# The second chunk's first pair of weight tiles as eight plain block products

## The chip, the cores and the metric

The kernel runs on one core of one Trainium2 chip. The metric is the device time of one execution in microseconds (us), lower is better. A core has five queues that run side by side: TensorE (PE, matmuls; its weight loads are a row of their own, PEld), VectorE (DVE), ScalarE (ACT), GpSimd (POOL) and SyncE (SP), which here issues every DMA transfer. Each runs its own instructions strictly in order and waits where an operand of another queue isn't ready.

## The reference

```python
q_s = np.exp(q - np.max(q, axis=-1, keepdims=True))      # then divided by its sum over the 64 features
k_s = np.exp(k - np.max(k, axis=2, keepdims=True))       # then divided by its sum over the 576 positions
kv = np.einsum('bhsd,bhse->bhde', k_s, v)                # 8 batches x 8 heads, 64 x 64 each
x = np.einsum('bhsd,bhde->bhse', q_s, kv)                # then seen as 4608 tokens x 512
a = x @ w_a                                              # 512 x 1536
b = x @ w_b
return (a * b @ w_out).astype(np.float32)                # 1536 x 512
```

q, k and v are float32; the three weights arrive as 64-bit floats.

## The kernel before, in words

**Tiles.** The tokens go through in nine chunks of 512. For each chunk, attention gives x, transposed (512 features x 512 tokens, four tiles of 128 features). d_ff = 1536 is cut into 12 blocks of 128 (f = 0 to 11) or six pairs (i = 0 to 5). For a pair, TensorE makes a and b (the gate products, line 535 of the profile, `product`), the product a\*b is formed by ACT and DVE, and is multiplied with the pair's rows of w_out (line 556, `project`), summed over all pairs in four accumulators `po`.

**Precision.** An operand is split into a high and a low part (`split`: ACT casts the high part at line 79, DVE subtracts it at line 82), and a product is three matmuls: high x high, high x low, low x high. The first chunk's w_out products (line 545, `project_first`) are single f32 matmuls.

**First chunk (c = 0).** It is computed plainly (line 510), while the weights are loaded, turned from 64-bit to f32 (`float_parts`: ACT, DVE, a POOL add at line 110, DVE), split, and put into scratch in device memory: the f32 tile of each half block as `dy`, and of three of a pair's four half blocks (A11, A12, A22: block f = 2i or 2i+1, first or second half of the 512 features) the split tile as `dw` (`keep_ab`, `put_w`).

**Later chunks.** A pair is made by Winograd's form of Strassen's scheme: x is cut into 2 x 2 blocks (B11, B21: first and second half of the features for the first half of the tokens; B12, B22 for the second), the weights into A11, A12, A21, A22, and seven products of sums replace eight. `x_operands` makes the sums of x (T1 to T4, tiles `xt`, lines 483 to 494) and splits all seven operands into tiles `xo`. `sums(i)` loads the four `dy` of a pair and makes the weight sums S1 to S4 on POOL (line 225). In chunk 1 the sums are split there and then, used, and put into `dw`; chunks 2 to 8 load all seven tiles of a pair from `dw` with `get_w` into eight buffers `ws`. The seven results are combined on DVE (tiles u2, u3, cc).

**Around the boundary of chunks 0 and 1.** `sums(0)` is called in chunk 0's last block, `sums(1)` at the start of chunk 1's pair 0. `x_operands` for chunk 1 goes through B11, T2, T3, T1, B21, B22, T4. The first PSUM banks of chunk 1 (k0 for `kx`, k1 for `ky` and `kp`) are those that the last gate products of chunk 0 (`pt`) leave: k0 is free after ACT's copy at line 517, k1 after DVE's product at line 521. In the same place an attention task for a later batch runs (`pm`, `mc`, `m`, `pmx`: a column maximum turned on TensorE and spread back, lines 261 to 276).

**What sets the order.** A scheduler of the language orders each queue when the program is built, from the order of the code, a timeline of its own and a few pinned places (`issue_after`, and the hand-written list of start steps). So an edit in one place can reorder instructions far from it.

Of the kernel before, what the change touches and what calls it, by code (L numbers as in the profile page):

```python
# [20 lines left out]

A11, S2, S3, S1, A12, S4, A22 = range(7)
B11, T2, T3, T1, B21, B22, T4 = range(7)
P1, P6, P7, P5, P2, P3, P4 = range(7)


# [1 line left out]
def linear_attention_then_gated_ffn(  # L30
# [162 lines left out]
    def keep_ab(f, half, y, w):  # L193
        i, r = divmod(f, 2)
        dy[i, r, half] = dr.tile([P, DM], F32, name=f"dy{i}{r}{half}")
        nc.sync.dma_start(out=dy[i, r, half], in_=y)
        op = ((A11, A12), (None, A22))[r][half]
        if op is not None:
            put_w(i, op, w)
        blocks[f, half] = w  # L200

# [4 lines left out]
    def get_w(i, op):  # L206
        w = ws_tile()
        nc.sync.dma_start(out=w.bitcast(F32), in_=dw[i, op].bitcast(F32))
        return w

    def sums(i):

        a = {}
        for r in range(2):
            for h in range(2):
                a[r, h] = sb.tile([P, DM], F32, name="ws_y", tag="wy", bufs=8)
                nc.sync.dma_start(out=a[r, h], in_=dy[i, r, h])
        sub, add = ALU.subtract, ALU.add
        for o, x, y, op in (
            ((1, 1), (1, 0), (1, 1), add),  # L220
            ((1, 0), (0, 0), (1, 0), sub),
            ((0, 0), (1, 1), (0, 0), sub),
            ((0, 1), (0, 1), (0, 0), sub),
        ):
            nc.gpsimd.tensor_tensor(out=a[o], in0=a[x], in1=a[y], op=op)
        return {S1: a[1, 1], S3: a[1, 0], S2: a[0, 0], S4: a[0, 1]}
# [249 lines left out]
    def x_operands(xf, which, box):  # L476

        b11, b12 = xf[:, 0:2, 0:H], xf[:, 0:2, H:T]
        b21, b22 = xf[:, 2:4, 0:H], xf[:, 2:4, H:T]
        for op in which:  # L480
            if op == T2:
                t1, t2 = t_tile(), t_tile()
                nc.vector.tensor_tensor(out=t1, in0=b12, in1=b11, op=ALU.subtract)
                nc.vector.tensor_tensor(out=t2, in0=b22, in1=t1, op=ALU.subtract)
                box["t1"], box["t2"] = t1, t2
                src = t2
            elif op == T3:
                src = t_tile()
                nc.vector.tensor_tensor(out=src, in0=b22, in1=b12, op=ALU.subtract)
            elif op == T1:  # L490
                src = box["t1"]
            elif op == T4:
                src = box["t2"]
                nc.vector.tensor_tensor(out=src, in0=b21, in1=src, op=ALU.subtract)
            else:
                src = {B11: b11, B21: b21, B22: b22}[op]
            o = xo_tile([P, 2, 2, H])
            split(o[:, 0], o[:, 1], src)
            box[op] = o
# [508 lines left out]
    for f in range(2, NF):  # L1008
        if 1 < f - 1 < NF - 3:
            tasks[f - 1][0]()  # L1010
        if f + 2 < NF:
            load_f(f + 2)

        with tc.issue_after(at["end", f - 2].ins):
            convert_wo(f)
            if f + 1 < NF:
                convert_ab(f + 1, 0)
                convert_ab(f + 1, 1)


        n = f - 3
        if n < 0:
            copies = ()
        else:
            copies = tasks[n][2]()
        if n + 1 < NF - 3:
            with tc.issue_after(startup[0]), tc.issue_after(at["end", max(f - 2, 1)].ins):
                tasks[n + 1][1]()
        if f == NF - 1:
            with tc.issue_after(at["end", f - 1].ins):  # L1030
                split_wo(0)
                split_wo(1)
            sy[0] = sums(0)
        if f > 2:
            pts = gate_banks(("k0", "k1"))
            for h in range(2):
                gate_part(f, x0, h, range(NP), pts[h])
                if h == 0:
                    with ExitStack() as pinned:
                        for copy in copies or ():  # L1040
                            pinned.enter_context(tc.issue_after(copy.ins))
                        at["ga", f] = gate_half(f, pts[0])
            at["end", f] = gate_end(at["ga", f], pts[1])
        if 0 <= n < len(tasks):
            tasks[n][3]()
        if f == NF - 2:
            x_operands(xfs[1], early + late, xo)
        project_first(*pending, po)
        pending = (f, at["ga", f])
    in_order((E.PE,), by_hand, len(traced))  # L1050
# [2 lines left out]
    def run_pending(last_only=False):  # L1053

        if not pend:
            return
        f, ghl, c, po = pend.pop(0)
        if c:
            project(f, ghl, po, c == NCH - 1 and f >= NF - 2)
        else:  # L1060
            project_first(f, ghl, po)
        if f == NF - 1:
            store(c, po)

    last = None
    for c in range(1, NCH):
        more = c + 1 < NCH
        attend = Spread(attention_tasks(c + 1) if more else [], 3 * NI - 3 - (1 if c == 1 else 0))
        po = None
        x, xo = xo, {}  # L1070
        for i in range(NI):
            def operand(op):
                if c > 1:
                    return get_w(i, op)
                if op in (A11, A12, A22):
                    return get_w(i, op)
                w = split_w(sy[i][op])
                put_w(i, op, w)
                return w

            if more and i == NI - 1:
                x_operands(xfs[c + 1], early, xo)
            kx = ps.tile([P, 2, H], F32, name="kx", tag="k0")
            ky = ps.tile([P, 2, H], F32, name="ky", tag="k1")
            ka = ps.tile([P, 2, H], F32, name="ka", tag="k2")
            cc = sb.tile([P, 4, 2, H], F32, name="cc", bufs=1)
            u2 = sb.tile([P, 2, H], F32, name="u2", bufs=1)
            u3 = sb.tile([P, 2, H], F32, name="u3", bufs=1)
            if c > 1 or i > 0:
                attend(last)  # L1090
            if c == 1:
                if i + 1 < NI:
                    sy[i + 1] = sums(i + 1)
                    split_wo(2 * i + 2)
                    split_wo(2 * i + 3)
            product(kx, operand(A11), x[B11], True)
            product(ky, operand(S2), x[T2], True)
            nc.scalar.copy(out=u2, in_=kx)  # L1098
            nc.vector.tensor_tensor(out=u2, in0=ky, in1=u2, op=ALU.add)  # L1099
            product(ka, operand(S3), x[T3], True)  # L1100
            last = nc.vector.tensor_tensor(out=u3, in0=ka, in1=u2, op=ALU.add)
            if more and i == NI - 1:
                x_operands(xfs[c + 1], late, xo)
            end = c == NCH - 1 and i == NI - 1
            if not end:
                run_pending()
            attend(last)
            kp = ps.tile([P, 2, H], F32, name="kp", tag="k1")
            product(kp, operand(S1), x[T1], True)
            product(kx, operand(A12), x[B21], False)  # L1110

            nc.vector.tensor_tensor(out=cc[:, 3], in0=kp, in1=u3, op=ALU.add)  # L1112
            nc.scalar.copy(out=cc[:, 0, 0], in_=kx[:, 0])  # L1113
            nc.vector.tensor_tensor(out=cc[:, 0, 0], in0=kx[:, 1], in1=cc[:, 0, 0], op=ALU.mult)
            last = nc.vector.tensor_tensor(out=cc[:, 3, 0], in0=cc[:, 3, 0], in1=cc[:, 3, 1], op=ALU.mult)
            if not end:
                run_pending()
            if po is None:
                po = [ps.tile([P, DM], F32, name=f"po{t}") for t in range(TT)]
            attend(last)  # L1120
            product(kp, operand(S4), x[B22], False)
            nc.vector.tensor_tensor(out=cc[:, 1], in0=kp, in1=u2, op=ALU.add)  # L1122
            nc.vector.tensor_tensor(out=cc[:, 1, 0], in0=cc[:, 1, 0], in1=cc[:, 1, 1], op=ALU.mult)  # L1123
            g1 = g_split(2 * i, cc[:, 0:2, 0])
            last_product = product(ka, operand(A22), x[T4], False)
            nc.vector.tensor_tensor(out=cc[:, 2], in0=ka, in1=u2, op=ALU.add)
            last = nc.vector.tensor_tensor(out=cc[:, 2, 0], in0=cc[:, 2, 0], in1=cc[:, 2, 1], op=ALU.mult)
            g2 = g_split(2 * i + 1, cc[:, 2:4, 0])
            pend += [(2 * i, g1, c, po), (2 * i + 1, g2, c, po)]
# [53 lines left out]
```

## Time and profile before

| | |
|---|---|
| runs | 973.65 us median of 3 (969.36 to 974.25) |
| profiled execution, first to last instruction | 970.9 us; what lies around it isn't recorded apart |
| TensorE busy | 941.8 us, 97% |
| VectorE, ScalarE, GpSimd busy | 631.3, 392.7, 104.2 us |
| DMA | 282.6 MB, mean 291 GB/s |
| chunk 0's last gate product starts its last 24 matmuls | 145.09 us |
| first matmul of chunk 1 | 155.17 us |
| first matmul of chunk 2 | 271.91 us |

Times within the execution count from the first instruction. In a timeline a row is a run of equal instructions: start, duration, engine, line, operation, output<-inputs, shapes, count, and in brackets the idle time before it and what ended it. A matmul's shown duration includes its way through the array; the pace of a row of matmuls is the distance of their starts. In the chain of waits a row's duration is that pace.

### The profile page before, as it was taken

The numbers are of one execution on the slowest core, as the hardware profiler recorded it, in microseconds if no ns is written. First come the engines' busy times: TensorE is split into PE (matmuls) and PEld (weight loads), VectorE is DVE, ScalarE is ACT, GpSimd is POOL, SyncE is SP. The second block draws the span as 40 slices with busy tenths as digits, with TensorE's granted clock in tenths as the row PEclk, the third lists the DMA queues.
The fourth block names the chain that finished last, engine by engine and source line by source line (L and its number), as shares of the span: only waits on it lengthen the run. The fifth ranks groups of instructions, "written<-read, shape, count | busy, mean of one in ns | idle before, by whom it ended". The sixth has DMA issues, their size and how long they took to land.

```text
span 970.9 us, 16970 instructions
## 1 busy us (share of the span) xinstructions
PE 941.8 (97%) x6159; PEld 844.9 (87%) x6159; DVE 631.3 (65%) x1249; ACT 392.7 (40%) x1085; POOL 104.2 (11%) x88
## 2 busy tenths in 40 slices
PE   5889998999999999999999999999999999999998
PEld 4656766899999999999999999999999999999997
DVE  7987878886686747665666657665766546553433
ACT  7787654543372416232443235223522263221101
POOL 1544343422000000000000000000000000000000
PEclk9999999999999999999999999999999999999999
DMA  9999585989998968997799779977998688767761
GB/s 347 411 383 377 203 291 183 410 308 344 302 347 274 373 232 274 302 378 245 255 332 358 260 251 334 322 268 256 337 296 289 240 299 269 275 226 273 255 208 59
DMA packets 97586, 282.60 MB, mean 291 GB/s; under 512 B 11680, under 2 KB 12256, under 8 KB 97504
## 3 DMA queue, kind: packets, MB, share of 16 engines
q1 hardware_dynamic: 97504, 281.52, 81.8%
q8 instruction: 49, 0.80, 0.3%
q14 instruction: 33, 0.27, 0.1%
HBM read 241.40 MB, written 37.98 MB: 288 GB/s over the span
## 4 chain that ended last, share of the span: by engine, by line
PE 87%; DVE 5%; DMA 2%; issue 2%; ACT 1%; POOL 1%; SPq 1%; DVEq 0%; POOLq 0%; ACTq 0%
PE po L556 27%; PE kp L535 14%; PE kx L535 14%; PE ka L535 13%; PE ky L535 7%; PE pk L312 3%; PE pt L510 3%; PE po L545 2%; PE px L466 2%; DMA raw<-in_w_ab 1%; POOL wr L110 1%; DMA mr<-dq 1%; DVE wy L113 1%; PE px L454 1%; DVE wo_w L82 0%
## 5 line engine op out<-in xcount | busy, mean ns | idle before, releaser
L556 PE MATMUL po<-wo_w,gh 128*128 128x512 f32 x768 | 231.0, 396 | 0.0
L535 PE MATMUL kx<-xo,ws 128*128 128x256 f32 x1152 | 164.7, 284 | 4.3 <-ACT ga L517 4.3
L556 PEld LDWEIGHTS po<-wo_w,gh 128*128 128x128 f32 x768 | 138.9, 189 | 26.4 <-ACT gh L79 0.3
L535 PE MATMUL ka<-xo,ws 128*128 128x256 f32 x1152 | 161.2, 283 | 0.0
L535 PE MATMUL kp<-xo,ws 128*128 128x256 f32 x1152 | 157.9, 284 | 1.4 <-DVE u L1099 1.4
L535 PEld LDWEIGHTS kx<-xo,ws 128*128 128x128 f32 x1152 | 151.0, 190 | 7.1 <-ACT ga L517 4.7
L535 PEld LDWEIGHTS ka<-xo,ws 128*128 128x128 f32 x1152 | 149.8, 188 | 3.9 <-issue 0.5
L535 PEld LDWEIGHTS kp<-xo,ws 128*128 128x128 f32 x1152 | 147.9, 190 | 3.9 <-issue 1.6
L556 PE MATMUL po<-wo_w,gl 128*128 128x512 f32 x384 | 140.1, 395 | 0.0
L79 ACT CAST gh<-cc 128x512 fp32r<-128x512 f32 x96 | 57.6, 621 | 135.6 <-DVE cc L1123 127.6
L1122 DVE TENSOR_TENSOR cc<-kp,u 128x512 f32<-128x512 f32 x48 | 33.2, 691 | 103.9 <-PE kp L535 103.9
L1113 ACT COPY cc<-kx 128x256 f32<-128x256 f32 x48 | 17.8, 372 | 189.4 <-PE kx L535 183.3
L556 PEld LDWEIGHTS po<-wo_w,gl 128*128 128x128 f32 x384 | 71.5, 188 | 16.4 <-DVE gl L82 0.4
L380 ACT ACTIVATE qt<-qt,st 128x64 f32<-128x64 f32 x224 | 75.0, 338 | 22.5 <-DVE st L377 16.3
L1112 DVE TENSOR_TENSOR cc<-kp,u 128x512 f32<-128x512 f32 x48 | 32.9, 686 | 73.3 <-PE kp L535 73.1
L535 PE MATMUL ky<-xo,ws 128*128 128x256 f32 x576 | 77.7, 284 | 0.6 <-DVE cc L1122 0.3
L535 PEld LDWEIGHTS ky<-xo,ws 128*128 128x128 f32 x576 | 72.0, 189 | 1.5 <-DVE cc L1122 0.5
L510 PE MATMUL pt<-xo,ws 128*128 128x512 f32 x288 | 70.3, 400 | 1.1 <-DVE ws L925 1.1
L82 DVE TENSOR_TENSOR gl<-cc,gh 128x512 fp32r<-128x512 f32 x96 | 65.4, 688 | 8.1 <-ACT gh L79 8.1
L510 PEld LDWEIGHTS pt<-xo,ws 128*128 128x128 f32 x288 | 53.5, 189 | 13.9 <-DVE ws L925 1.5
L244 POOL PARTITION_ALL_REDUCE mx<-m x20 | 14.4, 722 | 459.6 <-DVE m L255 432.1
L1098 ACT COPY u<-kx 128x512 f32<-128x512 f32 x48 | 28.0, 584 | 82.0 <-PE kx L535 82.0
(144 smaller groups left out, 1197.9 us busy)
## 6 DMA issues: line engine op xcount, KB each, us to landing
ws<-dw SPq DMA_DIRECT2D x312, 512.0 KB, 5.3
dw<-ws SPq DMA_DIRECT2D x42, 512.0 KB, 6.8
mr<-dq SPq DMA_DIRECT2D x112, 128.0 KB, 4.4
raw<-in_w_ab SPq DMA_DIRECT2D x24, 512.0 KB, 7.6
out<-ot SPq DMA_DIRECT2D x36, 256.0 KB, 4.6
vt<-in_v SPq DMA_DIRECT2D x28, 325.0 KB, 7.6
qt<-in_q SPq DMA_DIRECT2D x32, 256.0 KB, 5.2
kt<-in_k SPq DMA_DIRECT2D x24, 320.0 KB, 5.1
```

The lines of the kernel that those rows point to most:

```text
L79: nc.scalar.copy(out=hi, in_=src)
L82: return nc.vector.tensor_tensor(out=lo, in0=src, in1=hi.bitcast(F32), op=ALU.subtract)
L312: nc.tensor.matmul(pk, kt[:, j].rearrange("p h d -> p (h d)"), vt[:, j], start=(j == 0), stop=(j == J - 1),)
L380: nc.scalar.activation(out=qt[:, j, h], in_=qt[:, j, h], func=AF.Exp, bias=st[:, h, 0, j:j + 1], accum_out=st[:, h, 1, j:j + 1],)
L466: nc.tensor.matmul(px[:, s], w, m[:, s], start=(i == 0), stop=(i == 2))
L510: nc.tensor.matmul(pt, w[:, wp], x[g][:, xp], start=(g == 0 and i == 0), stop=(g == NP - 1 and i == 2),)
L535: ins = nc.tensor.matmul(pt[:, n], w[:, n, wp, c], x[:, xp, c], start=(first and n == 0 and i == 0), stop=(i == 5), skip_group_check=True,)
L545: nc.tensor.matmul(po[t], g[:, t * P:(t + 1) * P], wo_first[f], start=(f == 0), stop=(f == NF - 1),)
L556: ins = nc.tensor.matmul(po[t], a[:, ts], wo[f][:, w], start=(f == 0 and i == 0), stop=(f == NF - 1 and i == 2),)
L1098: nc.scalar.copy(out=u2, in_=kx)
L1112: nc.vector.tensor_tensor(out=cc[:, 3], in0=kp, in1=u3, op=ALU.add)
L1122: nc.vector.tensor_tensor(out=cc[:, 1], in0=kp, in1=u2, op=ALU.add)
```

## The change

- Pair 0 of chunk 1 is made by eight plain block products: A11·B11 + A12·B21, A11·B12 + A12·B22, A21·B11 + A22·B21 and A21·B12 + A22·B22, each result a\*b formed by a new helper `plain_gate` (ACT copies a, DVE multiplies with b).
- For that, A21's split tile of pair 0 is put into `dw` during chunk 0 as well and pair 0 loads four tiles with `get_w`; x needs an eighth operand, B12.
- `x_operands` for chunk 1 makes the plain blocks first (B11, B21, B12, B22) and the sums T2, T3, T1, T4 after.
- `sums(0)` is called in pair 4 of chunk 1, and the four weight sums of pair 0 are split and put into `dw` in pair 5, for chunks 2 to 8, which are computed as before.

```diff
-A11, S2, S3, S1, A12, S4, A22 = range(7)
-B11, T2, T3, T1, B21, B22, T4 = range(7)
+A11, S2, S3, S1, A12, S4, A22, A21 = range(8)
+B11, T2, T3, T1, B21, B22, T4, B12 = range(8)
...
-        op = ((A11, A12), (None, A22))[r][half]
-        if op is not None:
+        op = ((A11, A12), (A21, A22))[r][half]
+        if op != A21 or i == 0:
             put_w(i, op, w)
...
-                src = {B11: b11, B21: b21, B22: b22}[op]
+                src = {B11: b11, B12: b12, B21: b21, B22: b22}[op]
...
-            sy[0] = sums(0)
...
-            x_operands(xfs[1], early + late, xo)
+            x_operands(xfs[1], (B11, B21, B12, B22, T2, T3, T1, T4), xo)
...
+    def plain_gate(to, pt):
+
+        nc.scalar.copy(out=to[:, 0], in_=pt[:, 0])
+        return nc.vector.tensor_tensor(out=to[:, 0], in0=pt[:, 1], in1=to[:, 0], op=ALU.mult)
...
-            ky = ps.tile([P, 2, H], F32, name="ky", tag="k1")
+            ky = None if c == 1 and i == 0 else ps.tile([P, 2, H], F32, name="ky", tag="k1")
...
                 if i + 1 < NI:
                     sy[i + 1] = sums(i + 1)
+                if i + 2 == NI:
+                    sy[0] = sums(0)
+                if i + 1 < NI:
                     split_wo(2 * i + 2)
                     split_wo(2 * i + 3)
+                else:
+                    for op in (S2, S3, S1, S4):
+                        put_w(0, op, split_w(sy[0][op]))
+            if c == 1 and i == 0:
+                kp = ps.tile([P, 2, H], F32, name="kp", tag="k1")
+                w = get_w(i, A11)
+                product(kx, w, x[B11], True)
+                product(kp, w, x[B12], True)
+                w = get_w(i, A12)
+                product(kx, w, x[B21], False)
+                last = plain_gate(cc[:, 0], kx)
+                product(kp, w, x[B22], False)
+                last = plain_gate(cc[:, 1], kp)
+                run_pending()
+                attend(last)
+                po = [ps.tile([P, DM], F32, name=f"po{t}") for t in range(TT)]
+                g1 = g_split(0, cc[:, 0:2, 0])
+                w1, w2 = get_w(i, A21), get_w(i, A22)
+                product(ka, w1, x[B11], True)
+                product(ka, w2, x[B21], False)
+                last = plain_gate(cc[:, 2], ka)
+                kx = ps.tile([P, 2, H], F32, name="kx", tag="k0")
+                attend(last)
+                product(kx, w1, x[B12], True)
+                product(kx, w2, x[B22], False)
+                last = plain_gate(cc[:, 3], kx)
+                g2 = g_split(1, cc[:, 2:4, 0])
+                pend += [(0, g1, c, po), (1, g2, c, po)]
+                continue
```

The scheduler makes other queues of it. Three places, each before and with the change.

**TensorE at the boundary of chunks 0 and 1**, from chunk 0's last gate products (`pt`) on. Before:

```order
L510 MATMUL pt_1411<-xo,ws 128x512 x12
L510 MATMUL pt_1412<-xo,ws 128x512 x12
L535 MATMUL kx<-xo,ws 128x256 x12
L271 MATMUL pmx<-m_1391,ones 128x128
L545 MATMUL po_492<-wo_w,ga 128x512
```

With the change:

```order
L510 MATMUL pt_1404<-xo,ws 128x512 x12
L510 MATMUL pt_1405<-xo,ws 128x512 x12
L535 MATMUL kx<-xo,ws 128x256 x13
L271 MATMUL pmx<-m_1396,ones 128x128
L545 MATMUL po_494<-wo_w,ga 128x512
L545 MATMUL po_495<-wo_w,ga 128x512
L545 MATMUL po_496<-wo_w,ga 128x512
L545 MATMUL po_497<-wo_w,ga 128x512
L535 MATMUL kx<-xo,ws 128x256 x4
L535 MATMUL kp<-xo,ws 128x256 x12
```

The attention task's `pmx` stands behind the first 12 matmuls of `kx` before, and behind 13 now.

**VectorE in the same place**, from the product that frees k1 for chunk 0's last gate. Before:

```order
L521 TENSOR_TENSOR ga<-pt_1314,ga 128x512
L82 TENSOR_TENSOR wo_w<-yo_344,wo_w 128x512
L82 TENSOR_TENSOR wo_w<-yo_350,wo_w 128x512
L484 TENSOR_TENSOR xt<-xf,xt 128x512
L489 TENSOR_TENSOR xt<-xf 128x512
L82 TENSOR_TENSOR xo<-xt,xo 128x512 x2
L494 TENSOR_TENSOR xt<-xf,xt 128x512
L82 TENSOR_TENSOR xo<-xt,xo 128x512
L82 TENSOR_TENSOR wo_w<-wo_w 128x512
L263 TENSOR_REDUCE mc<-pm 128x1
L82 TENSOR_TENSOR xo<-xf,xo 128x512 x2
```

Behind these stand one more `xo` split and the `m` that `pmx` reads. With the change:

```order
L82 TENSOR_TENSOR wo_w<-yo_344,wo_w 128x512
L82 TENSOR_TENSOR wo_w<-yo_350,wo_w 128x512
L484 TENSOR_TENSOR xt<-xf,xt 128x512
L489 TENSOR_TENSOR xt<-xf 128x512
L82 TENSOR_TENSOR xo<-xf,xo 128x512 x3
L82 TENSOR_TENSOR xo<-xt,xo 128x512 x2
L82 TENSOR_TENSOR wo_w<-wo_w 128x512
L263 TENSOR_REDUCE mc<-pm 128x1
L82 TENSOR_TENSOR xo<-xt,xo 128x512
L494 TENSOR_TENSOR xt<-xf,xt 128x512
L265 TENSOR_SCALAR m_1396<-ident,mc 128x128
```

Twelve subtractions stand ahead of `m` in both; the three splits of B21, B12 and B22 moved ahead of those of the sums, and the sum for T4 (line 494) behind them. ACT's copy that frees k0 (line 517) stands behind the cast of T4 before, and ahead of it now. POOL's queue reads the same in both: the 24 adds of line 225 stand in one row, of which the first four are now pair 1's.

**TensorE at the boundary of chunks 1 and 2**, where `px` is the last attention product of chunk 2 and `ky`, `ka` are its first gate products that need sums of x. Before:

```order
L466 MATMUL px<-qh,kvl_1994 128x384
L535 MATMUL kx<-xo,ws 128x256 x7
L556 MATMUL po_1594<-wo_w,gh_2767 128x512 x2
L556 MATMUL po_1595<-wo_w,gh_2767 128x512 x2
L556 MATMUL po_1596<-wo_w,gh_2767 128x512 x2
L556 MATMUL po_1597<-wo_w,gh_2767 128x512 x2
```

After these follow 16 more `po` matmuls and then `ky`. With the change:

```order
L556 MATMUL po_1559<-wo_w,gl_2804 128x512
L466 MATMUL px<-qh,kvh_1909 128x128
L466 MATMUL px<-ql,kvh_1909 128x128
L466 MATMUL px<-qh,kvl_1910 128x128
L466 MATMUL px<-qh,kvh_1977 128x384
L466 MATMUL px<-ql,kvh_1977 128x384
L466 MATMUL px<-qh,kvl_1978 128x384
L535 MATMUL ky<-xo,ws 128x256
L535 MATMUL ka<-xo,ws 128x256
```

All 24 `po` matmuls stood between `px` and `ky` before; none does now.

Beside these, in chunk 0 the two small VectorE operations that end an attention task's sum (lines 321 and 323) stood behind a weight split and an integer shift for f = 4, and now stand directly behind line 320 and one gate product.

## Prediction

> **What bounds the kernel now.** I read the page first, then TensorE's waits over the whole span, then the chain of waits and the timelines at the places that these name. The page:
>
> ```profile
> PE 941.8 (97%) x6159; PEld 844.9 (87%) x6159; DVE 631.3 (65%) x1249; ACT 392.7 (40%) x1085; POOL 104.2 (11%) x88
> PE 87%; DVE 5%; DMA 2%; issue 2%; ACT 1%; POOL 1%; SPq 1%; DVEq 0%; POOLq 0%; ACTq 0%
> ```
>
> TensorE is busy for 97% of the span and holds 87% of the chain. So an added matmul costs its whole pace, and a gain must come from the few places where TensorE waits. All its waits behind chunk 0's start that bear on the change, from the waits of TensorE (engine and line, what it waited for, us in total, times, longest):
>
> ```profile
> PE kx L535 <- ACT ga L517: 4.3, 1, 4.3
> PE pkb L299 <- DVE wholes L323: 1.7, 1, 1.7
> PE kp L535 <- DVE u L1099: 1.4, 1, 1.4
> PE pm L261 <- DVE m L255: 0.5, 1, 0.5
> PE ky L535 <- DVE cc L1122: 0.3, 1, 0.3
> ```
>
> Four of the five lie at the boundary of chunks 0 and 1 (155 to 182 us): 4.3 + 1.4 + 0.5 + 0.3 = 6.5 us of idle time. The chain gives the pace of a product (12 matmuls) there:
>
> ```profile
> 155.17 2.93 PE kx L535 x12
> 161.93 1.42 PE ky L535 x12
> 182.09 2.90 PE kp L535 x12
> ```
>
> A product takes 1.42 us, but 2.93 and 2.90 behind the two idle stretches: half speed, 1.5 us lost each time. The boundary costs 6.5 + 3.0 = **9.5 us**, all that the change can win there.
>
> Why the wait: VectorE and GpSimd over the same time, from their timelines.
>
> ```profile
> 141.45 13.08 POOL L225 TENSOR_TENSOR ws_y<-ws_y 128x512 f32<-128x512 f32 x8 [4.48 <-DMA qt<-in_q]
> 141.53 3.42 DVE L82 TENSOR_TENSOR wo_w<-yo,wo_w 128x512 fp32r<-128x512 f32 x2
> 146.56 1.78 DVE L489 TENSOR_TENSOR xt<-xf 128x512 f32<-128x512 f32 x1
> 151.66 1.75 DVE L494 TENSOR_TENSOR xt<-xf,xt 128x512 f32<-128x512 f32 x1
> 155.00 0.68 DVE L82 TENSOR_TENSOR wo_w<-wo_w 128x512 fp32r<-128x512 f32 x1
> 157.61 0.28 DVE L265 TENSOR_SCALAR m<-ident,mc 128x128 f32<-128x128 f32 x1
> ```
>
> While GpSimd makes eight weight sums (141.45 to 154.53), VectorE's subtractions of two SBUF tiles take 1.7 us of pace instead of 0.6: eight of them lose 8 x 1.09 = 8.7 us. ACT's cast of T4 waits for line 494, and the copy that frees k0 (line 517) waits behind that cast.
>
> **The change part by part.**
>
> *One more product.* Eight instead of seven: 12 matmuls, **+1.4 us**, on the path for certain.
>
> *The first wait.*
>
> ```profile
> 145.09 5.83 PE L510 MATMUL pt<-xo,ws 128*128 128x512 f32 x24
> 154.54 0.57 ACT L517 COPY ga<-pt 128x512 f32<-128x512 f32 x1
> ```
>
> ACT now copies k0 free ahead of T4's cast. It needs line 489 (done 148.3), two casts at 0.58 and its copy of 0.57: 150.1, before chunk 0's last gate product ends (145.09 + 5.8 = 150.9). So `kx` starts at once, and 13 matmuls run until 152.4. Then `pmx` stands in the queue, and it reads `m`. In VectorE's queue twelve subtractions stand ahead of `m`, as many as before. What is late next is `m`.
>
> ```profile
> 158.03 0.46 PE L271 MATMUL pmx<-m,ones 128*128 128x128 f32 x2
> 158.33 1.88 PE L545 MATMUL po<-wo_w,ga 128*128 128x512 f32 x4
> 267.96 1.75 ACT L79 CAST xo<-xt 128x512 fp32r<-128x512 f32 x3 [0.83 <-DVE xt L484]
> ```
>
> GpSimd's sums don't leave this place: its queue still has 24 adds in a row; the first eight are now those of pairs 1 and 2. If eight again fall on the twelve subtractions, `m` comes at 157.6 as in the row and `pmx` at 158.0: an idle stretch of 5.6 us. With one set of four sums in that time it is 157.6 - 4 x 1.09 = 153.2, idle 1.2 us; with none, 12 x 0.6 + 0.4 behind 141.6 is 149.2, idle 0. I take 5.6, since the nearest row has eight and GpSimd's queue order didn't change. Behind it the half speed follows: 1.5. So this place costs 7.1 us where the first wait cost 4.3 + 1.5 = 5.8; bounds 0 to 7.1. `po`, `kx` and `kp` are queued behind `pmx`; `kp` also needs k1, which VectorE frees two operations behind `m`, at 159.2, while TensorE comes to `kp` at 158.2 + 3.4 or later: no further wait.
>
> [...]
>
> *The second wait* (1.4 + 0.5 + 0.3, and 1.5 at half speed: 3.7 us). TensorE waits there for VectorE, which works without a pause (9.77 of 10 us, the third number with a count):
>
> ```profile
> 170.00:180.00 10.00, 9.57 (x79) 9.15 (x77) 9.77 (x22) 6.56 (x34) 5.74 (x4) 1.00 1.03 406
> ```
>
> Of VectorE's work the change takes out two sums `u`, three sums `cc` and four weight splits of pair 0, nine operations of 0.6, and adds one split (B12): 4.8 us less against 2.2 us of waiting. Pair 1's sums and splits now come first and are ready early. I take the whole **-3.7**; the other bound is 0.
>
> Loads: pair 0 now needs four tiles by 150 to 165 us, where pair 0's loads are issued from 133.9 us on (line 208, from 125 to 185 us). One is 512 KB:
>
> ```profile
> L208 SPq DMA_DIRECT2D ws<-dw x7: 319/371/969, 133.9 to 179.6; - x7
> DMA to landing us min/median/max: 3.3/6.6/8.2
> ...
> ws<-dw SPq DMA_DIRECT2D x312, 512.0 KB, 5.3
> 20.00:60.00 40.00, 36.99 (x155) 26.01 (x154) 39.55 (x64) 31.20 (x58) 19.02 (x13) 0.98 1.03 404
> 100.00:120.00 20.00, 20.00 (x81) 13.74 (x80) 16.35 (x28) 14.43 (x37) 8.99 (x6) 1.00 0.51 199
> ```
>
> With a cover of some 15 us, about twice the longest landing of 8.2, the loads cost nothing; without it, one landing, 5.3 to 6.6.
>
> *Start.* A21's tile is one more write of 512 KB while DMA moves 404 GB/s at a share of 1.03 (last two numbers): 1.3 us of DMA time. Behind 100 us DMA has slack (199 GB/s at 100 to 120 us), so between 0 and 1.3 reaches TensorE; I take 0.5. On the other side, `wholes` moves ahead of a split and a shift:
>
> ```profile
> 67.81 0.67 DVE L82 TENSOR_TENSOR ws<-wy,ws 128x512 fp32r<-128x512 f32 x1
> 68.41 0.41 DVE L107 TENSOR_SCALAR wo_raw<-wy 128x512 int32<-128x512 int32 x1
> 68.82 0.67 DVE L82 TENSOR_TENSOR ws<-wy,ws 128x512 fp32r<-128x512 f32 x1
> 69.41 0.34 DVE L323 SCALAR_TENSOR_TENSOR wholes<-pk,den,mask 128x128 f32<-128x128 f32 x1
> 69.89 0.30 PE L299 MATMUL pkb<-ident,kt 128*128 128x128 f32 x1 [1.69 <-DVE wholes L323]
> ```
>
> 0.6 + 0.35 + 0.6 = 1.5 earlier, of the 1.7 that TensorE waits. Start: **-1.0**, bounds -1.7 and +1.3.
>
> *Boundary of chunks 1 and 2.* Before, 24 matmuls cover the way from the last `px` to `ky`:
>
> ```profile
> 265.34 0.34 PE L466 MATMUL px<-qh,kvl 128*128 128x384 f32 x1
> 266.34 2.02 PE L556 MATMUL po<-wo_w,gh 128*128 128x512 f32 x8
> 271.91 0.28 PE L535 MATMUL ky<-xo,ws 128*128 128x256 f32 x1
> 266.04 0.68 DVE L658 TENSOR_TENSOR xf<-px,mr 128x512 f32<-128x512 f32 x1
> 267.24 0.68 DVE L484 TENSOR_TENSOR xt<-xf,xt 128x512 f32<-128x512 f32 x1
> ```
>
> With the change they stand ahead of `px`, and the way is bare: `px`'s tail 0.2, line 658 0.7, line 484 0.7, ACT's cast 0.6, hand-overs 0.1, then `ka` one cast later, 0.5 less a matmul of 0.1. **+2.7**. The order of the queues excludes a gain; bounds 1.9 (without `ka`'s part and the slack between) and 4.2 (half speed behind it).
>
> *Weight sums at the chunk's end.* Four more splits on ACT and VectorE, 1 MB of loads, 2 MB of writes:
>
> ```profile
> 240.00:260.00 20.00, 20.00 (x137) 18.66 (x136) 14.47 (x25) 6.12 (x11) 0.00 (x0) 1.00 1.00 327
> ```
>
> VectorE and ACT have room (14.5 and 6.1 of 20 us); DMA has no slack there (share 1.00), but the sums move these bytes here from 130 to 175 us, they do not add them. I take 0; if the cover is gone, see the third rival.
>
> Sum: 1.4 + (7.1 - 5.8) - 3.7 + 2.7 - 1.0 = **+0.7 us** on a span of 970.9: 971.6. The median of the runs shown lies 2.75 above this span, and I carry that over: 973.65 + 0.7 = **974.3**. A measurement of this kernel can tell about 0.5%, 4.9 us, from no change: 968.8 to 978.5 counts as none.
>
> **The rivals.**
>
> *The first wait goes for good.* The four tile loads now stand between pair 1's and pair 2's operands of the sums, so the second set of sums may come so late that the subtractions get through between the sets. Then 7.1 falls to 0: +0.7 - 7.1 = -6.4, **967.3**. For it: a megabyte more ahead of the last operand, 3.4 us at the 290 GB/s of the page. Against: a set moved later still falls on subtractions that are left.
>
> *One set in the way.* Idle 1.2, half speed 1.5: 7.1 falls to 2.7, -3.7, **970.0**. What speaks for it and against is the same, with only a part of the shift.
>
> *The chunk's end decides, and it is slower.* The four sums take four of the eight `ws` buffers at the start of pair 5, and a buffer is free only when its write has landed:
>
> ```profile
> dw<-ws SPq DMA_DIRECT2D x42, 512.0 KB, 6.8
> ```
>
> Then a tile of pair 5 can be fetched four tiles ahead, not eight: three products and a `po` group, 3 x 1.42 + 2.8 = 7.1 us, against 6.8 for the write that frees a buffer and 5.3 for the load, 12.1. It decides if a product waits for a buffer that a write holds: 12.1 - 7.1 = 5.0 late, +5.7, **979.4**. Against: five products and two groups lie ahead of the first tile that follows a write, and SP's queue is in an order that was laid out with this in it.
>
> **How the numbers follow.** Forecast 0.50 (its own range 971 to 977.5), one set 0.16, first wait gone 0.20, chunk's end 0.14. Faster by over 0.5%: the gone wait nearly whole, 0.18, and a little of one set, 0.01. Slower by over 0.5%: most of the chunk's end, 0.13, and 0.01 of the forecast with half speed at the second boundary. Same: 0.67. The range runs from just below the gone wait to just under the chunk's end, 967 to 979.
>
> **What would show it.** `kx` at about 150.9 behind chunk 0 without a wait; a wait of `pmx` for `m` in its place, then half speed; no wait of `kp` for `u` some 25 us later; `ky` of chunk 2 waiting about 2 us for an ACT cast; no wait of a product for a load in chunk 1. Wrong it is if `pmx` doesn't wait (first two rivals), if `pkb` waits as before or a `pt` waits for a split, or if a wait for `ws` shows in pair 5.

## The result, and the profile after

The changed kernel takes **982.58 us** (median of 4, 979.56 to 984.49), the kernel before 973.69 us: a ratio of 1.0104, 95% interval 1.0081 to 1.0127 (the quotient of the two medians, 1.0091, lies inside it). The forecast was 974.3 with a range of 967 to 979. It was wrong: the change costs 8.9 us.

The profiled execution has a span of 977.8 us against 970.9, so it shows 6.9 of the 8.9 us. It is the fastest of the four runs shown; their median lies 4.8 us above this span, against 2.75 before. The remaining 2 us are in no trace.

TensorE's waits with the change (engine and line, what it waited for, us in total, times, longest):

```profile
PE pmx L271 <- DVE m L265: 4.3, 1, 4.3
PE pka L299 <- ACT kt L293: 2.5, 1, 2.5
PE ky L535 <- ACT xo L79: 2.2, 1, 2.2
PE pkb L299 <- DVE wholes L323: 1.1, 1, 1.1
PE pq L441 <- DVE qt L367: 1.0, 1, 1.0
PE ka L535 <- DVE cc L1162: 0.7, 1, 0.7
```

`kx` no longer waits and neither does `kp`; `pmx` and chunk 2's `ky` do. The stretches behind three of these waits, with the granted clock third from the right:

```profile
91.00:96.00 5.00, 4.83 (x17) 3.92 (x18) 1.99 (x5) 3.63 (x7) 2.63 (x2) 0.66 0.86 340
...
158.00:160.00 2.00, 1.74 (x4) 1.25 (x5) 2.00 (x4) 0.13 (x1) 1.76 (x2) 0.50 0.00 0
160.00:162.00 2.00, 2.00 (x3) 0.69 (x3) 0.69 (x3) 1.92 (x4) 0.00 (x0) 0.50 0.00 0
162.00:164.00 2.00, 2.00 (x4) 0.73 (x3) 0.65 (x2) 0.36 (x1) 0.00 (x0) 0.50 0.62 229
...
278.00:280.00 2.00, 2.00 (x11) 2.00 (x11) 2.00 (x5) 0.77 (x2) 0.00 (x0) 0.50 0.94 361
```

The page shows these as busy time: from 160 to 162 us TensorE is busy for 2.00 of 2.00 us, at a granted clock of 0.50. They must be read from the clock, not from the waits.

The boundary of chunks 0 and 1, from the timelines of TensorE, VectorE and GpSimd:

```profile
146.65 5.82 PE L510 MATMUL pt<-xo,ws 128*128 128x512 f32 x24
152.30 1.70 PE L535 MATMUL kx<-xo,ws 128*128 128x256 f32 x13
158.26 0.77 PE L271 MATMUL pmx<-m,ones 128*128 128x128 f32 x2 [4.25 <-DVE m L265]
158.82 6.18 PE L545 MATMUL po<-wo_w,ga 128*128 128x512 f32 x8
146.58 5.17 DVE L82 TENSOR_TENSOR xo<-xf,xo 128x512 fp32r<-128x512 f32 x3
156.83 1.29 DVE L265 TENSOR_SCALAR m<-ident,mc 128x128 f32<-128x128 f32 x1
144.63 6.58 POOL L225 TENSOR_TENSOR ws_y<-ws_y 128x512 f32<-128x512 f32 x4 [7.03 <-DMA ws_y<-dy]
152.92 6.92 POOL L225 TENSOR_TENSOR ws_y<-ws_y 128x512 f32<-128x512 f32 x4 [1.72 <-DVE xo L82]
```

Both sets of four sums fall on VectorE's work again: six subtractions take 1.56 to 1.76 us each (0.68 for a single one that isn't stretched), `m` itself 1.29 (0.28 before), `m` ends at 158.1, and `pmx` waits. The `po` group behind it takes 6.18 us where the same group at full speed takes 3.60.

And the boundary of chunks 1 and 2:

```profile
271.02 1.10 PE L556 MATMUL po<-wo_w,gl 128*128 128x512 f32 x4
273.64 0.33 PE L466 MATMUL px<-qh,kvl 128*128 128x384 f32 x1
276.13 0.39 PE L535 MATMUL ky<-xo,ws 128*128 128x256 f32 x1 [2.16 <-ACT xo L79]
277.12 2.55 PE L535 MATMUL ky<-xo,ws 128*128 128x256 f32 x11
```

The way from the last `px` to `ky` is 2.5 us long, about as forecast. But the last `px` itself ends at 274.0, where it ended at 265.7 before, so TensorE ran out of `po` matmuls first; and the half speed follows (11 matmuls of `ky` in 2.55 us, 1.46 before).

| place | forecast | in the profiles |
|---|---|---|
| start, up to chunk 0's last 24 gate matmuls (145.09, now 146.65) | -1.0 | +1.6 |
| first wait: idle and half speed, 5.8 before | 7.1 (+1.3) | 4.25 + 2.9 = 7.2 (+1.4) |
| one more product | +1.4 | +1.4 |
| second wait, 3.7 before | -3.7 | -3.7 |
| boundary of chunks 1 and 2 (what is left of 6.9) | +2.7 | +6.2 |
| sum | +0.7 | +6.9 |

The 2.9 is 6.18 - 3.60 of the `po` group and 0.77 - 0.46 of `pmx`. The last row isn't read from one place: it is what the others leave of 6.9, and holds 0.7 us of a wait of `ka` in chunk 2 as well.

### The profile page after: what moved, and what is told of

Same layout as the page of the kernel before. It is cut to its first block, busy times and chain, and to the rows that moved or that the text cites. A ratio compares the mean times of both kernels' runs of the same rounds, so it can differ in the third digit from the quotient of the medians.

```text
span 977.8 us, 16988 instructions
## 1 busy us (share of the span) xinstructions
PE 947.1 (97%) x6171; PEld 846.9 (87%) x6171; DVE 630.9 (65%) x1245; ACT 394.4 (40%) x1088; POOL 103.9 (11%) x88
## 4 chain that ended last, share of the span: by engine, by line
PE 77%; DMA 9%; DVE 4%; issue 4%; POOL 3%; ACT 1%; SPq 0%; POOLq 0%; DVEq 0%; ACTq 0%
PE po L556 25%; PE kx L535 13%; PE ka L535 13%; PE kp L535 13%; PE ky L535 7%; PE pk L312 3%; POOL wr L110 2%; DMA wo_raw<-in_w_out 2%; PE px L466 2%; DMA dy<-wy 1%; DMA vt_first<-in_v 1%; DMA dw<-ws 1%; PE po L545 1%; DMA qt<-in_q 1%; DMA mr<-dq 1%
```

## The experiments

Each time has the kernel before beside it, run on the same chip; medians in us. The changed kernel was not run again in these sessions, in which the kernel before took 972.6 to 973.3 us (973.7 beside the changed kernel), so a difference to its 982.58 holds to about 1 us.

### GpSimd's additions left out

```diff
-            nc.gpsimd.tensor_tensor(out=a[o], in0=a[x], in1=a[y], op=op)
+            None if i in (1, 2) else nc.gpsimd.tensor_tensor(out=a[o], in0=a[x], in1=a[y], op=op)
```

> The changed kernel with the eight GpSimd additions of the weight sums of pairs 1 and 2 left out (the raw tiles are split and used in their place; this leaves out part of the computation). Loads, splits and products stay. Theory (GpSimd's additions slow VectorE's subtractions of two SBUF tiles, so `m` comes late): the subtractions between 144 and 157 us take 0.7 us each instead of up to 1.76, `m` (line 265) is done by about 151 us, `pmx` waits less than 0.5 us instead of 4.3, and the half speed behind it (3.7 us) is gone: 982.6 - 8 = 974.6. Rival (the twelve operations ahead of `m` in VectorE's queue, or its operands, make it late by themselves): `pmx` waits 3 us or more and the time is 981 to 983.

Measured: **974.67**, before 973.27; ratio 1.0014 (0.9995 to 1.0033). That is 7.9 us less than the changed kernel. VectorE in this run:

```profile
146.04 1.89 DVE L82 TENSOR_TENSOR xo<-xf,xo 128x512 fp32r<-128x512 f32 x3
151.06 0.28 DVE L265 TENSOR_SCALAR m<-ident,mc 128x128 f32<-128x128 f32 x1
```

The three splits take 1.89 us, not 5.17, and `m` ends at 151.3, not 158.1. `pmx` is gone from the list of waits. So the additions are the cause of that wait, not the number of operations ahead of `m`. In the profiles 7.0 us are won by the end of the `po` group behind `pmx` (157.4, and 164.4 with the additions), but only 3.5 are left over the whole span: part goes again later, where `px` now waits 2.9 us (0.4 with the additions). The medians differ by 7.9, since the changed kernel's profile lies below its median, as said above. With the additions a subtraction takes 5.17 / 3 = 1.72 us, beside 6.58 / 4 = 1.65 us an addition, and without them 1.89 / 3 = 0.63. By what mechanism the additions do this no run here shows.

### A21's put alone

```diff
-        op = ((A11, A12), (None, A22))[r][half]
-        if op is not None:
+        op = ((A11, A12), (A21, A22))[r][half]
+        if op != A21 or i == 0:
```

(in the kernel before; nothing else.)

> The kernel before with one edit: A21's split tile of pair 0 is put into scratch too (512 KB, used by nobody); chunk 1's pair 0 stays Strassen, its sums stay where they were. With this edit alone the scheduler also reorders TensorE at the boundary of chunks 1 and 2: the `po` matmuls of pair 4 stand ahead of the last `px`, as in the changed kernel, but the eight transfers of the moved sums are not there. Theory A (the start is slowed by this put and the reordering that it sets off): chunk 0's last 24 gate matmuls begin at 146.6 us like in the changed kernel, not at 145.1. Rival (the start is slowed by x_operands' new order): 145.1. At the boundary of chunks 1 and 2, theory B (the last rows of the attention task land late because the transfers of the moved sums lie ahead of them): `px` is done at about its old place and `ky` waits some 2 us at most, 1.5 at half speed behind it. Rival (the new order of TensorE alone makes the loss): `ky` and what surrounds it lose 6 to 7 us here too. Time: 973.7 + 1.5 + 2 to 3.5 = 977 to 979 by A and B, 982 by the rival of B.

Measured: **980.27**, before 973.27; ratio 1.0073 (1.0049 to 1.0097). A write of 512 KB that nobody reads makes 7.0 us. Two of its waits, and the first and last of the eight matmuls of the last kind of `px` (duration min, median, max; start of the first and last):

```profile
PE pka L299 <- ACT kt L293: 2.6, 1, 2.6
PE ky L535 <- ACT xo L79: 2.2, 1, 2.2
```

```profile
L466 PE MATMUL px<-qh,kvl x8: 273/306/338, 248.6 to 272.2; 128*128 128x128 f32 x4, 128*128 128x384 f32 x4
```

The same view of the kernel before, and of the changed kernel:

```profile
L466 PE MATMUL px<-qh,kvl x8: 272/306/337, 240.1 to 265.3; 128*128 128x128 f32 x4, 128*128 128x384 f32 x4
```

```profile
L466 PE MATMUL px<-qh,kvl x8: 274/307/337, 246.5 to 273.6; 128*128 128x128 f32 x4, 128*128 128x384 f32 x4
```

So theory B fell: `px` is about as late as with the whole change, though none of the moved sums' transfers is there. What the put changes is the scheduler's order: chunk 2's attention tasks begin 8.5 us later from their first `px` on. In TensorE's timelines that first `px` stands behind 444 gate matmuls and 99 `po` matmuls of chunk 1, and behind 397 and 85 before; at a pace of 1.42 / 12 and 2.77 / 12 us these 61 matmuls are 5.6 + 3.2 = 8.8 us. So the place in the queue is enough for the delay. Theory A fell for this profile: chunk 0's last 24 gate matmuls begin at 145.0 us as before, since the half speed behind the wait for line 293 didn't come (last section).

### No sums at chunk 1's end

```diff
-                    return get_w(i, op)
+                    return get_w(1 if i == 0 and op in (S1, S2, S3, S4) else i, op)
...
-                if i + 2 == NI:
-                    sy[0] = sums(0)
                 if i + 1 < NI:
...
-                else:
-                    for op in (S2, S3, S1, S4):
-                        put_w(0, op, split_w(sy[0][op]))
```

> The changed kernel without the weight sums of pair 0 at chunk 1's end: no loads, additions, splits or writes of them; chunks 2 to 8 load pair 1's sum tiles in their place (this leaves out part of the computation, with as many transfers in chunks 2 to 8). The last `px` then stands ahead of 24 `po` matmuls again. Theory (the sums' transfers at 228 to 260 us make the attention rows late, and with the new order of TensorE this costs some 6.5 us at the boundary of chunks 1 and 2): no wait of `ky`, 982.6 - 6.5 = 976. Rival (the loss at that boundary has another cause, such as fewer free buffers or the length of chunk 1): a wait of 2 us or more stays there, 980 to 983.

Measured: **974.37**, before 973.27; ratio 1.0018 (1.0003 to 1.0032), 8.2 us less than the changed kernel. `ky` doesn't wait:

```profile
L466 PE MATMUL px<-qh,kvl x8: 275/306/337, 244.2 to 265.3; 128*128 128x128 f32 x4, 128*128 128x384 f32 x4
```

The first `px` is late here too (244.2), but the last is in time: the four come every 7.0 us, and every 9.0 in the changed kernel. The 3 MB of loads and writes that are missing here may be why; the scheduler's order is another one too (7.9 us with the put alone and none of these transfers), so that part isn't separated. What is shown is that the loss doesn't need these transfers (the put alone has it).

### `px` pinned ahead of the `po` group

```diff
+                with ExitStack() as pinned:
+                    if c == 1 and i == NI - 1: pinned.enter_context(tc.issue_after(at["xp"].ins))
                     run_pending()
```

(`at["xp"]` is the last matmul of the last `px`.)

> The changed kernel, all its work and transfers kept, with one pin: the first `po` group of chunk 1's pair 5 is scheduled behind the last `px`. Theory (the operand rows of `px` land late, at about 270 us, so the order of TensorE is an answer to it and not the cause): `px` now waits itself, 4 to 6 us, and nothing is won: 981 to 984. Rival (the order of TensorE is the cause): the waits of `ky` go, 982.6 - 5 = 977.6 or less.

Measured: **988.67**, before 973.27; ratio 1.0151 (1.0115 to 1.0188), 6 us more than the changed kernel, beyond what either theory gave.

```profile
PE px L466 <- ACT qh L79: 6.6, 2, 3.6
```

TensorE's order, on which the forecast's +2.7 rested, isn't the cause: with `px` ahead of the `po` group TensorE waits longer, for operands that come late.

### One call fewer for the attention tasks

```diff
-        attend = Spread(..., 3 * NI - 3 - (1 if c == 1 else 0))
+        attend = Spread(..., 3 * NI - 3 - (2 if c == 1 else 0))
```

> The changed kernel with chunk 1's attention tasks spread over 13 calls, not 14, so that each task is called somewhat earlier; all work, transfers and the start kept. Theory (the rows of the last attention task are late because the whole chain of attention tasks of chunk 1 is laid late, each waiting for the buffer of the one but last): the first `px` begins some 6 us earlier, `ky` doesn't wait, 982.6 - 6 = 976.6. Rival (the moved sums' transfers ahead of them in the queue make the rows late however early they are called): `px` or `ky` waits 4 us or more, 981 to 984. The wait of `pmx` for `m` stays at 4.3 by both.

Measured: **973.42**, before 972.93; ratio 1.0003 (0.9993 to 1.0012), 9.2 us less than the changed kernel, with every transfer and product kept.

```profile
PE pmx L271 <- DVE m L265: 5.4, 1, 5.4
```

```profile
229.92 0.22 PE L466 MATMUL px<-qh,kvh 128*128 128x128 f32 x1
...
258.76 0.34 PE L466 MATMUL px<-qh,kvl 128*128 128x384 f32 x1
```

The first `px` begins 16 us earlier than in the changed kernel, the last ends at 259.1. `ky` is gone from the list of waits. `pmx` still waits, longer by 1.1 us, since TensorE comes to it earlier. In the profiles 7.8 us are won, 2.3 of them up to the `po` group behind `pmx` and 5.5 behind it. The late attention tasks are so shown to be the cause at this boundary: called earlier, they are done in time even with the moved sums.

### The sums of x pinned behind `m`, and both mends together

```diff
-            x_operands(xfs[1], (B11, B21, B12, B22, T2, T3, T1, T4), xo)
+            x_operands(xfs[1], (B11, B21, B12, B22), xo)
...
+    with tc.issue_after(at["m"].ins):
+        x_operands(xfs[1], (T2, T3, T1, T4), xo)
```

> The changed kernel with the sums T2, T3, T1, T4 of x and their splits pinned behind `m` in VectorE's queue, all of GpSimd's additions kept. `m` then has seven subtractions ahead of it, not twelve. Theory (both together make `m` late: GpSimd's additions stretch the subtractions, and their number ahead of `m` says how often): with four stretched by 1.1 us `m` is done by 152.5 us, `pmx` doesn't wait over 1 us, and no half speed follows: 982.6 - 7 = 975.6. Rival (the T operands now come late for pair 1, or another wait takes the place of this one): the wait goes but as much appears within chunk 1, 980 to 983.

> The two edits before together: T sums pinned behind `m`, 13 calls. If the two losses are apart in time and have apart causes, the gains add: 982.6 - 6 - 7 = 969.6, 3 to 4 us below the kernel before (973.3), with only the product, the start's 1.5 us and little else left against it. Rival (they share a cause, the load of VectorE or of the transfer queue in chunk 1): less than half of the second gain, 974 to 977.

Measured: **980.85** (before 972.93; ratio 1.0081, 1.0066 to 1.0097) for the first, **972.41** (ratio 0.9993, 0.9981 to 1.0005) for both. The gain of pinning is 1.7 us alone and 1.0 beside the earlier calls, where 7 were expected. A wait and VectorE in the first:

```profile
PE kp L535 <- DVE ga L521: 3.4, 1, 3.4
```

```profile
150.13 0.29 DVE L265 TENSOR_SCALAR m<-ident,mc 128x128 f32<-128x128 f32 x1
152.65 1.76 DVE L489 TENSOR_TENSOR xt<-xf 128x512 f32<-128x512 f32 x1
158.91 0.68 DVE L521 TENSOR_TENSOR ga<-pt,ga 128x512 f32<-128x512 f32 x1
```

`m` comes at 150.4 and `pmx` doesn't wait. But line 521, which frees k1 for `kp`, stood two operations behind `m`, and the stretched subtractions are now between them. The queue was reordered and not made shorter, so the next product in it waits. This is the rival of the expectation. (In the second the same wait is 3.6 us.)

### A21 split again, and the buffer that this takes

Pair 0 reads A21's f32 tile and splits it; no put in chunk 0:

```diff
-        if op != A21 or i == 0:
+        if op != A21:
...
+                y21 = sb.tile([P, DM], F32, name="ws_y", tag="wy", bufs=8)
+                nc.sync.dma_start(out=y21, in_=dy[0, 1, 0])
...
+                a21 = split_w(y21)
...
-                w1, w2 = get_w(i, A21), get_w(i, A22)
+                w1, w2 = a21, get_w(i, A22)
```

> The changed kernel without A21's put in chunk 0: pair 0 loads A21's f32 tile (256 KB, written anyway) at the boundary of chunks 0 and 1 and splits it there, one cast and one subtraction more. With this the scheduler's start order is the kernel before's again, and the last `px` of chunk 1 stands ahead of `po` matmuls again, with the moved sums' transfers kept. Theory C (the one put changes the scheduler's order from the start on, and the loss at the boundary of chunks 1 and 2 comes with that order, not with the moved sums' bytes): chunk 0's last 24 gate matmuls begin at 145.1 us, the boundary of chunks 1 and 2 loses 2 us or less, 982.6 - 1.5 - 5 = 976; if GpSimd's additions also come at another time and `pmx` no longer waits, 968 to 970. Rival D (the moved sums' transfers make that loss): the start is won, the boundary still loses 5 us or more, 980 to 982.

Measured: **966.86**, before 972.93; ratio 0.994 (0.9926 to 0.9953): 15.7 us less than the changed kernel and 6.1 less than the kernel before. TensorE's wait, GpSimd, and `px`:

```profile
PE pmx L271 <- DVE m L265: 0.4, 1, 0.4
```

```profile
140.85 6.32 POOL L225 TENSOR_TENSOR ws_y<-ws_y 128x512 f32<-128x512 f32 x4 [3.60 <-DMA ws_y<-dy]
157.59 4.35 POOL L225 TENSOR_TENSOR ws_y<-ws_y 128x512 f32<-128x512 f32 x3 [10.41 <-DMA ws_y<-dy]
```

```profile
L466 PE MATMUL px<-qh,kvl x8: 274/304/339, 236.0 to 260.2; 128*128 128x128 f32 x4, 128*128 128x384 f32 x4
```

The second set of sums starts at 157.6, when `m` has long been done (152.9), and the attention tasks begin 10 us earlier than in the changed kernel, with the moved sums in place. Most of these 10 us are what the first wait and the start no longer cost: in TensorE's queue the first `px` stands only some 20 gate matmuls further ahead. Why the second set is late was tested by moving one tile:

```diff
-                y21 = sb.tile([P, DM], F32, name="ws_y", tag="wy", bufs=8)
+                y21 = sb.tile([P, DM], F32, name="y21", tag="u2", bufs=1)
```

> The run that splits A21 again (966.9 us), with one change of place: A21's f32 tile lies in the buffer of u2, which pair 0 no longer uses, and not in one of the eight buffers from which the weight sums take theirs. All else as there. Theory (there the second set of GpSimd's sums came at 157.6 us, behind `m`, only because that tile held a buffer; so the first wait was won by the buffer): with the buffer free the second set starts by 150 us, VectorE's subtractions are stretched to 1.7 us again ahead of `m`, `pmx` waits 2 to 4.5 us and half speed may follow: 970 to 975. Rival (the first wait was won by something else in that kernel, such as the earlier start): `pmx` waits less than 1 us and the time stays at 966 to 968.

Measured: **973.96**, before 972.59; ratio 1.0016 (1.0005 to 1.0026).

```profile
PE pmx L271 <- DVE m L265: 4.6, 1, 4.6
```

```profile
139.99 5.99 POOL L225 TENSOR_TENSOR ws_y<-ws_y 128x512 f32<-128x512 f32 x4 [3.16 <-DMA ws_y<-dy]
147.25 6.71 POOL L225 TENSOR_TENSOR ws_y<-ws_y 128x512 f32<-128x512 f32 x4 [1.27 <-DVE xt L489]
```

With eight buffers free the second set starts at 147.25, on the subtractions, and 7.1 us are lost again. So the first wait was won by a buffer being held.

### The same buffer held in the kernel before

```diff
+                if i == 0:
+                    hold = sb.tile([P, DM], F32, name="ws_y", tag="wy", bufs=8)
+                    nc.sync.dma_start(out=hold, in_=dy[0, 1, 0])
                 if i + 1 < NI:
                     sy[i + 1] = sums(i + 1)
...
+            if c == 1 and i == 0:
+                nc.vector.tensor_copy(out=sb.tile([P, 1], F32, name="den"), in_=hold[:, 0:1])
```

> The kernel before, seven products and all sums where they were, with one edit: a spare f32 tile is loaded into one of those eight buffers ahead of the sums of pair 1 and is read (one column, VectorE) only after the first `run_pending` of pair 0, so that the second set of GpSimd's sums starts later. Theory (four sums fewer fall on the subtractions: 4 x 1.09 = 4.4 us less on VectorE): `kx` starts at about 151 us without its 4.3 us and without half speed, 1.5: 973 - 5.8 = 967; the waits of `kp` and `pm` at 180 us stay. Rival (the same sums now fall on the splits of pair 0's weight sums, so the second wait grows by as much): 971 to 974. What it is short of the eight products' run says what these are worth by themselves.

Measured: **967.50**, before 972.59; ratio 0.9947 (0.9929 to 0.9964).

```profile
PE kp L535 <- DVE u L1102: 1.4, 1, 1.4
PE pm L261 <- DVE m L255: 0.5, 1, 0.5
```

```profile
152.02 1.66 PE L535 MATMUL kx<-xo,ws 128*128 128x256 f32 x12
```

`kx` starts without a wait and at full speed; the second wait stays. That the time is so near the forecast 967 is partly luck: chunk 0's last 24 gate matmuls begin 1.3 us later than before (146.4), and the half speed behind the second wait is missing (12 matmuls of `kp` in 1.66 us, 2.90 before; mean granted clock of the profile 0.998, 0.994 before), though the waits are the same. The seven-product kernel with a held buffer (0.9947) can't be told from the eight-product kernel with one (0.994). So the eight products by themselves bring nothing that these runs can tell; what takes back their gain at the second wait wasn't separated.

### Two more combinations

> The run that splits A21 again, with the attention tasks spread over 13 calls too. Theory (the boundary of chunks 1 and 2 is already mended there, its `px` begins in time): 966 to 968, no difference. Rival (the 2 to 3 us that `px` and `ka` still wait at 238 to 258 us come from late tasks too): 964 to 965.

Measured: **966.35**, before 972.59; ratio 0.9937 (0.9919 to 0.9955), no difference to the run without the earlier calls (0.994). It has the lowest median of all; the edits are those shown above. The changed kernel with the put kept, the held buffer (read ahead of pair 0's first `run_pending`) and the earlier calls was the last:

> The changed kernel, A21's put and its start kept, with the two mends together that keep all the work: a spare f32 tile held in one of the eight buffers until pair 0's first `run_pending` (the second set of GpSimd's sums comes later) and 13 calls for the attention tasks. Theory (the changed kernel's loss consists of the wait for `m` with the half speed behind it, about 8, the late attention tasks, about 9, and the start, about 1.5): the first two go, 982.6 - 17 = 965.6, and with the put's start kept it lies 0 to 2 us above the run that splits A21 again (966.9): 965.5 to 969. `pmx` waits less than 1 us, `ky` of chunk 2 not at all. Rival (as with T behind `m`, another wait takes the place of the one for `m`, or the put costs more than the start): 971 to 975.

Measured: **971.38**, before 972.75; ratio 0.9987 (0.9973 to 1.0002). 11.2 us of the expected 17 came.

```profile
PE ky L535 <- DVE cc L1162: 2.8, 1, 2.8
PE pka L299 <- ACT kt L293: 2.6, 1, 2.6
```

```profile
152.27 11.29 POOL L225 TENSOR_TENSOR ws_y<-ws_y 128x512 f32<-128x512 f32 x8 [13.38 <-DMA ws_y<-dy]
```

All sums are behind `m` now and `pmx` doesn't wait, but a `ky` of chunk 1 waits 2.8 us for a combination on VectorE, a wait of a length that no other run shows there. (The profiled execution took 974.9 us, 3.5 above the median, so the others may not have all of this.) Each edit gives the scheduler another order, so gains found one by one need not add. How much the put costs beyond the late tasks and the start stays open.

## Why the prediction was wrong

**What bounds the kernel: right.** Nearly every loss found lies in a wait of TensorE at one of the places named (start, first wait, boundary of chunks 1 and 2), or in the half speed behind it.

**The added product and the second wait: right.** The matmuls of `kx`, `ky`, `ka` and `kp` are 12 more, `kp` waits for no `u`, `pm` for no `m`. Of the 3.7, only the 2.2 of idle time are sure: the run with the held buffer has the same waits and no half speed behind them.

**The first wait: right in its mechanism, and in its sum by luck.** `kx` starts at once, and `pmx` waits for `m`, since the sums fall on the subtractions. But the idle stretch is 4.25 and not 5.6: `m` is done about when forecast, and TensorE, late from the start, comes to `pmx` 1.6 us later. The half speed costs 2.9 and not 1.5, since it lasts until about 164 us, not 3 us. The two errors cancel. (With one call fewer for the attention tasks TensorE isn't late, and the stretch is 5.4 us.) The rivals "gone" and "one set" didn't come true here. But their mechanism, a second set of sums too late to matter, is what the run that splits A21 again shows. That it takes 966.9, where the forecast for "gone" was 967.3, is chance: it has neither the put nor the loss at the second boundary.

**The start: wrong sign.** `pkb` starts 2.1 us earlier:

```profile
67.76 0.30 PE L299 MATMUL pkb<-ident,kt 128*128 128x128 f32 x1 [1.07 <-DVE wholes L323]
```

But only 0.6 of that is a shorter wait for `wholes`; 1.5 come from `pk` ahead of it, which waits 0.5 us for ACT's line 300 and waited 1.9 before. And the gain wasn't followed up. `pka` then waits 2.5 us for ACT's line 293, where it waited 1.6, so 1.2 of the 2.1 are left. The half speed behind that wait takes 1.6 (24 `pt` matmuls in 7.39 us, not 5.83), and a new wait of `pq` for line 367 takes 1.0. The step took a wait for won where a later one on the conversion of the weights (VectorE, ACT, GpSimd and DMA) gives part of it back, and it had no half speed behind that one. Without that half speed the start costs nothing (the 24 gate matmuls begin at 145.0 us with A21's put alone).

**The boundary of chunks 1 and 2: the step that failed most.** It priced the bare way from `px` to `ky` and left `px` where it was. The order of the queue at the boundary was taken as the cause; it was the sign of something earlier. By its last kind of matmul the first `px` already starts 6.4 us later than before (240.1, now 246.5), and the last 8.3. The rows (`mr`) that the attention tasks load for their operands show the same. SP issues them, between 200 and 275 us, from and to (line 421; before, then with the change):

```profile
L421 SPq DMA_DIRECT2D mr<-dq x16: 445/587/596, 221.7 to 251.8; - x16
```

```profile
L421 SPq DMA_DIRECT2D mr<-dq x16: 451/592/1691, 216.5 to 262.5; - x16
```

The last is issued 10.7 us later. With A21's put alone it is issued at 262.3, and at 248.4 in the run with one call fewer. The forecast read TensorE's queue at the boundary, and not the place of the first `px` in it some 30 us ahead (behind 397 gate and 85 `po` matmuls of chunk 1 before, 443 and 99 now), nor SP's issues of the rows. So the boundary loses 6.2 us where the step had 2.7. Its upper bound, 4.2, held the half speed but no later `px`. Why the scheduler lays the tasks later once A21's tile is put stays open.

**The third rival: right in sign and place, wrong in mechanism.** Slower, by work at chunk 1's end, was given 0.14 and 979.4. But no product of pair 5 waits for a `ws` load; it was the attention's operands that came late.

**Median from span.** 2.75 us was carried over. With the change it was 4.8, since the profiled execution was the fastest.

## What to carry to other kernels

Where a scheduler lays the queues, an edit's cost isn't at the edit: a write that nobody reads cost 7 us, and what the traces show of it is a new order of work far behind it. Compare each queue for work that is needed later and now begins later, before pricing what stands where. The stall that GpSimd's additions made on VectorE here (1.72 us a subtraction, 0.63 without them) was mended by when the additions may run, by one held buffer (5 us in one kernel, 7 in the other), and not by reordering VectorE's queue, which handed the wait, 3.4 us long, to the next product.

## What the runs showed of the hardware beside that

**The half speed came behind some waits and not behind others of the same length, and had no fixed price.** Nine of these kernels wait 2.5 to 2.6 us for line 293. Behind it four profiles show half speed for some 3 us (granted clock 0.66 to 0.72 over 5 us) and four don't (1.00); for the ninth, with `px` pinned, it isn't shown. One with half speed, then one without, over the same stretch:

```profile
91.00:96.00 5.00, 4.84 (x17) 3.92 (x18) 1.99 (x5) 3.60 (x7) 2.64 (x2) 0.66 0.84 334
```

```profile
91.00:96.00 5.00, 4.86 (x24) 4.08 (x25) 1.99 (x5) 4.02 (x8) 2.67 (x2) 1.00 0.88 347
```

(the first without GpSimd's additions, the second with A21's put alone). The wait of `ky` for the cast of `xo`, 2.16 us long in both, has half speed behind it in the changed kernel (11 matmuls in 2.55 us) and none with A21's put alone (granted clock 1.00 from 274 to 280 us). Nor did it always begin where the wait ended. With `px` pinned, the wait for `m` ended at 156.4:

```profile
156.00:157.00 1.00, 0.57 (x3) 0.52 (x4) 1.00 (x3) 0.30 (x1) 0.92 (x2) 1.00 0.00 0
157.00:158.00 1.00, 1.00 (x3) 0.38 (x2) 1.00 (x2) 0.00 (x0) 1.00 (x1) 0.68 0.00 0
158.00:160.00 2.00, 2.00 (x4) 0.81 (x3) 0.69 (x2) 1.75 (x4) 0.02 (x1) 0.50 0.00 0
```

The matmuls first run at the full clock and are halved from about 157.3 on. In the kernel before, half speed follows a wait of 1.4 us (12 matmuls of `kp` in 2.90 us), and none follows one of 1.7 us (24 `pt` matmuls at 69.95 us in 5.84). What decides it no run here shows. For a sum, the half speed behind a wait of some microseconds cost 0 to 2.9 us in these profiles, and this spread belongs in the range of the forecast.
